# Sliding-window attention and SwiGLU on one core: scores of two heads on the two row halves of the array, 65-column products by 128 keys, in half-head steps

## Chip, cores, metric

One core of one Trainium2 chip. The metric is the device time of one execution in microseconds (us); lower is better. In the profiled runs the time is about 1.7 us more than the span of the profile. Engines in the profile: PE is the TensorE matmul, PEld its weight load, DVE VectorE, ACT ScalarE, POOL GpSimd, SP SyncE.

## The reference

```python
# q, k, v: (8 batches, 8 heads, 576 positions, 64)
scores = q @ k^T / 8;  keep 0 <= query - key < 64, else -1e9
x = softmax(scores) @ v                    # per head, then (4608 tokens, 512)
out = (silu(x @ w_gate) * (x @ w_val)) @ w_out   # 512 -> 1536 -> 512, f32
```

## The kernel before

Tokens go through in groups of 128 (36 groups, g); four groups make a tile t of 512 tokens for the gate and value matmuls. A batch has 576 positions, so every ninth half-group of 64 begins a sequence. All matmuls use bf16 operands, except the turns (transposes through the array) of keys and queries, which the profile shows as f32. Exp needs no running maximum; the row sum comes from a column of ones beside the values.

The attention part. Keys are stored block-diagonally: 64 keys of head a of a pair in rows and columns 64a to 64a+63. One matmul then makes the scores of 64 keys of both heads, with the whole array. The values are block-diagonal too, so that a product has 130 output columns (two heads of 64 and two sums).

```python
    def scores(g):
        E = Es[g % ER]
        m = 2 * g
        ...
        for h in range(2):
            s_ps = ps_a.tile([P, 2, 4, 64], FP32, name="s_ps", tag="a")
            for i in range(2):
                p = 2 * h + i
                nc.tensor.matmul(s_ps[:, i, 0], keys(m + 1, p), queries(m + 1, p))
                nc.tensor.matmul(s_ps[:, i, 1:3], keys(m, p), queries(m, p, 2))
                if g:
                    nc.tensor.matmul(s_ps[:, i, 3], keys(m - 1, p), queries(m, p))
            e = E[:, 1:21].rearrange("r (p y) x -> r p y x", y=5)[:, 2 * h:2 * h + 2, 0:hi, :]
            act.activation(e, s_ps[:, :, 0:hi, :], AF.Exp, scale=0.125)
            dve.tensor_mul(e, e, mk[:, 0:hi].unsqueeze(1).to_broadcast([P, 2, hi, 64]))
```

`ps_a` is a PSUM pool of three one-bank tiles, shared by scores, products, and the turns `tp` (keys, queries) and `xtp` (attention output, the x turns). The gate and value sums have two banks each, the projection one.

`gv` makes the gate and value sums of one of twelve column blocks; its `finish` on DVE comes one step later and frees those two banks:

```python
    def finish(state):
        g_ps, v_ps, th, t, m, c0, n = state
        sg = fsb.tile([P, 512], FP32, name="sg", tag="sg")
        dve.scalar_tensor_tensor(sg[:, 0:n], th[:, 0:n], 1.0, g_ps[:, 0:n], ALU.add, ALU.mult)
        dve.tensor_mul(hT[t][:, m, c0:c0 + n], sg[:, 0:n], v_ps[:, 0:n])
```

The loop, one pass per group, after a written-out prologue that ends with a projection and one more group's attention (cuts: loads and casts):

```python
    flush()
    project(0, 3)
    products(11)
    turn_q(6)
    scores(12)
    turn_x(11)
    ...
    turn_k(7)
    for w in range(8, NG):
        ...
        step(t, 3 * s)                # gv of a block, then finish of the block before
        if w + 4 < NG:
            products(w + 4)
        ...
        step(t, 3 * s + 1)
        if w + 5 < NG:
            scores(w + 5)
        if w + 4 < NG:
            turn_x(w + 4)
        ...
        step(t, 3 * s + 2)
        ...                           # turn_k or turn_q, in turn
        project(t - 1, s)
```

The softmax here doesn't subtract the row's maximum and nothing guards it: scores larger than these inputs give would overflow.

## Time and profile before

| | before |
|---|---|
| time, median of 2 runs | 388.3 us (388.06 to 388.54) |
| span of the profiled run (its own time was 391.72) | 390.0 us |
| PE busy | 364.8 us, 94% |
| DVE, ACT, POOL busy | 67%, 44%, 24% |
| period of the loop, per group | 9.57 us |

The first lines are from the page of the kernel before: busy time of each engine, and the granted matmul clock in 40 slices of the span, in tenths. Then two of its groups of instructions: line, engine, operation, operands, count, then busy us and mean ns of one.

```profile
PE 364.8 (94%) x2524; PEld 209.2 (54%) x2566; DVE 262.1 (67%) x520; ACT 173.1 (44%) x296; POOL 94.5 (24%) x120
...
PEclk9859969999999999999999999999999999999999
...
L162 DVE TENSOR_TENSOR E<-E,mask 128x512 bf16<-128x512 bf16 (+1 forms) x72 | 42.1, 589 | 24.0 <-ACT E L161 21.9
...
L161 ACT ACTIVATE E<-s_ps 128x512 bf16<-128x512 f32 (+1 forms) x72 | 38.7, 594 | 13.9 <-PE s_ps L159 13.0
```

The mean ns of a PE matmul is its latency; matmuls overlap, and the pace is read from the starts. The chain of waits does that. These are lines of the chain of the kernel before, in order of time (start us, us, what), for a little more than one group in the loop.

```profile
212.27 0.86 PE g_ps L235 x4
...
214.00 0.68 PE ao_ps L180 x12
214.68 0.86 PE g_ps L235 x4
...
216.25 0.19 PE s_ps L156
...
216.86 0.22 PE xtp L199 x4
...
218.81 0.44 PE tp L111 x4
219.25 2.59 PE o_ps L252 x12
221.84 0.86 PE g_ps L235 x4
```

One group takes 221.84 - 212.27 = 9.57 us, and nothing but PE stands in the chain. Twelve products take 0.68 us, so 56.6 ns each; the scores take 0.45 us (in the timeline of PE, from the first score at 216.25 us to the first x turn at 216.70; the first score piece of this chain is longer because one value matmul before it is missing from the records). In the stretch from 165 to 300 us PE is busy 134.11 of 135 us. The loop starts at about 117 us; before it the core waits for loads, then for chains of Exp, mask and finish.

### The profile page before, as it was taken

What the parts mean: (1) busy time and instruction counts of PE and PEld (TensorE: products, weight loads), DVE (VectorE), ACT (ScalarE), POOL (GpSimd) and SP (SyncE); (2) the same over time, 40 slices, a digit from 0 to 9 for tenths busy, and PEclk for the clock granted to TensorE, in tenths of its full rate; (3) what the DMA queues carried; (4) which work ended last, traced back from release to release, by engine and by line L of the source; (5) the groups of instructions that cost most, each with busy time, mean ns of one, the idle gap of its engine ahead of it and who ended that gap; (6) DMA issues with size and microseconds to landing.
All of it is one profiled execution on the core that took longest, in us unless ns stands there. A gap on an engine that the chain in (4) does not pass through costs nothing.

```text
span 390.0 us, 6619 instructions
## 1 busy us (share of the span) xinstructions
PE 364.8 (94%) x2524; PEld 209.2 (54%) x2566; DVE 262.1 (67%) x520; ACT 173.1 (44%) x296; POOL 94.5 (24%) x120
## 2 busy tenths in 40 slices
PE   8679698988879999999999999999999999999995
PEld 3464355766655555555555555555555555544442
DVE  6857777856666777675777686768777766664530
ACT  2265539534354454544343434343545444423321
POOL 3702342702145222222222222222222200000000
PEclk9859969999999999999999999999999999999999
DMA  9979999518741525253626352636263100000112
GB/s 204 301 224 233 312 341 208 120 54 165 174 109 44 134 82 134 83 134 89 141 90 141 83 137 85 137 86 143 86 145 85 48 28 29 27 29 28 54 54 83
DMA packets 88320, 47.62 MB, mean 122 GB/s; under 512 B 39136, under 2 KB 82144, under 8 KB 88288
## 3 DMA queue, kind: packets, MB, share of 16 engines
q1 hardware_dynamic: 88288, 47.20, 48.5%
q8 instruction: 20, 0.33, 0.4%
q14 instruction: 12, 0.10, 0.1%
HBM read 37.75 MB, written 9.44 MB: 121 GB/s over the span
## 4 chain that ended last, share of the span: by engine, by line
PE 81%; DVE 8%; DMA 4%; ACT 3%; issue 2%; SPq 1%; POOL 1%; ACTq 0%; POOLq 0%; DVEq 0%
PE o_ps L252 24%; PE g_ps L235 21%; PE v_ps L235 21%; PE ao_ps L180 5%; PE tp L111 4%; DMA k_f<-in_k_dram 2%; PE xtp L199 2%; PE s_ps L157 2%; DVE E L162 2%; ACT E L161 2%; DMA v_f<-in_v_dram 1%; DVE x_b L185 1%; PE s_ps L156 1%; DVE kbd L120 1%; PE s_ps L159 1%
## 5 line engine op out<-in xcount | busy, mean ns | idle before, releaser
L235 PE MATMUL g_ps<-xT,wg 128*128 128x512 bf16 (+1 forms) x457 | 111.6, 358 | 5.9 <-DVE sg L246 3.9
L235 PE MATMUL v_ps<-xT,wv 128*128 128x512 bf16 (+1 forms) x473 | 112.3, 359 | 0.9 <-DVE hT L247 0.5
L240 ACT ACTIVATE th<-g_ps 128x512 f32<-128x512 f32 (+1 forms) x120 | 67.5, 562 | 83.7 <-DVE x_b L185 44.6
L252 PE MATMUL o_ps<-wo,hT 128*128 128x512 bf16 x420 | 96.5, 379 | 0.7
L246 DVE SCALAR_TENSOR_TENSOR sg<-th,g_ps 128x512 f32<-128x512 f32 (+1 forms) x120 | 75.3, 628 | 17.1 <-ACT th L240 16.6
L247 DVE TENSOR_TENSOR hT<-sg,v_ps 128x512 bf16<-128x512 f32 (+1 forms) x120 | 76.1, 634 | 9.7 <-PE ao_ps L180 0.5
L235 PEld LDWEIGHTS <-wv 128*128 128x128 bf16 x480 | 47.1, 98 | 48.4 <-issue 2.2
L252 PEld LDWEIGHTS <-hT 128*128 128x128 bf16 x432 | 42.2, 98 | 45.4
L235 PEld LDWEIGHTS <-wg 128*128 128x128 bf16 x480 | 44.7, 98 | 40.0 <-issue 7.2
L162 DVE TENSOR_TENSOR E<-E,mask 128x512 bf16<-128x512 bf16 (+1 forms) x72 | 42.1, 589 | 24.0 <-ACT E L161 21.9
L104 POOL CAST k_fw<-k_f 128x1024 bf16<-128x1024 f32 x17 | 23.0, 1353 | 125.9 <-DMA k_f<-in_k_dram 87.0
L132 POOL CAST vbd<-v_f 64x512 bf16<-64x512 f32 x72 | 45.6, 634 | 24.1 <-DMA v_f<-in_v_dram 20.7
L184 DVE RECIPROCAL r<-ao_ps 128x4 f32<-128x4 f32 x72 | 12.8, 177 | 51.3 <-PE ao_ps L180 51.2
L161 ACT ACTIVATE E<-s_ps 128x512 bf16<-128x512 f32 (+1 forms) x72 | 38.7, 594 | 13.9 <-PE s_ps L159 13.0
L104 POOL CAST q_fw<-q_f 128x1024 bf16<-128x1024 f32 x17 | 23.2, 1362 | 60.2 <-DMA q_f<-in_q_dram 46.5
L180 PE MATMUL ao_ps<-vbd,E 128*128 128x130 bf16 x428 | 32.5, 226 | 3.7 <-DVE E L162 2.3
L180 PEld LDWEIGHTS <-E 128*128 128x128 bf16 x428 | 28.0, 100 | 12.9 <-DVE E L162 4.0
L185 DVE TENSOR_TENSOR x_b<-ao_ps,r 128x256 bf16<-128x256 f32 x72 | 30.6, 425 | 2.5
L120 DVE COPY kbd<-tp 64x1024 bf16<-64x1024 bf16 x36 | 24.6, 684 | 3.8 <-PE tp L111 3.5
L200 ACT COPY xT<-xtp 128x512 bf16<-128x512 bf16 x36 | 21.3, 591 | 8.5 <-PE xtp L199 8.4
L126 ACT COPY qT<-tp 128x1024 bf16<-128x1024 bf16 x18 | 18.2, 1012 | 13.2 <-PE tp L111 13.2
L156 PE MATMUL s_ps<-qT,kbd 128*128 128x64 bf16 x144 | 20.1, 197 | 3.8 <-ACT qT L126 1.8
(75 smaller groups left out, 216.2 us busy)
## 6 DMA issues: line engine op xcount, KB each, us to landing
v_f<-in_v_dram SPq DMA_DIRECT2D x32, 256.0 KB, 5.3
k_f<-in_k_dram SPq DMA_DIRECT2D x12, 512.0 KB, 4.3
q_f<-in_q_dram SPq DMA_DIRECT2D x12, 512.0 KB, 5.0
w_f<-in_moe_w_gate_dram SPq DMA_DIRECT2D x6, 512.0 KB, 7.1
w_f<-in_moe_w_val_dram SPq DMA_DIRECT2D x6, 512.0 KB, 7.2
wo_f<-in_moe_w_out_dram SPq DMA_DIRECT2D x6, 512.0 KB, 6.7
k_f<-in_k_dram SPq DMA_DIRECT2D x4, 384.0 KB, 4.7
q_f<-in_q_dram SPq DMA_DIRECT2D x4, 384.0 KB, 5.5
```

What stands on the lines that cost most here:

```text
L104: eng.tensor_copy(y, x_f[:])
L120: dve.tensor_copy(kbd[n % KR][h, :, :, 64 * a:64 * a + 64], tp[h].rearrange("r p (b x) -> r p b x", x=64),)
L132: eng.tensor_copy(vbd[n % VR][64 * a:64 * a + 64, c:4:2, :, 64 * a:64 * a + 64], v_f[64 * c:64 * c + 64, :, a:8:2, :],)
L161: act.activation(e, s_ps[:, :, 0:hi, :], AF.Exp, scale=0.125)
L162: dve.tensor_mul(e, e, mk[:, 0:hi].unsqueeze(1).to_broadcast([P, 2, hi, 64]))
L180: nc.tensor.matmul(o_ps[:, i, :], w, x, start=(n == 0), stop=(n == len(parts) - 1))
L185: dve.tensor_mul(x_b[:, 256 * h:256 * h + 256].rearrange("r (p a d) -> r p a d", p=2, a=2), o_ps[:, :, 0:P].rearrange("r p (a d) -> r p a ...
L235: nc.tensor.matmul(ps[:, 0:n], w[:, c, P * m:P * m + P], xT[t][:, c, c0:c0 + n], start=(c == 0), stop=(c == 3),)
L240: act.activation(th[:, 0:n], g_ps[:, 0:n], AF.Tanh, scale=0.5)
L246: dve.scalar_tensor_tensor(sg[:, 0:n], th[:, 0:n], 1.0, g_ps[:, 0:n], ALU.add, ALU.mult)
L247: dve.tensor_mul(hT[t][:, m, c0:c0 + n], sg[:, 0:n], v_ps[:, 0:n])
L252: nc.tensor.matmul(o_ps[:], hT[t][:, c, P * s:P * s + P], wo[:, c, :], start=(c == 0), stop=(c == 11),)
```

## The change

The intent: use row tiling. The keys of a head lie on 64 rows, and two heads of a pair can be multiplied at the same time on the upper and the lower 64 rows of the array, without zeros in between. The scores then come with 128 keys of one head on the partitions, so a product needs two matmuls of 65 columns per head, in place of three of 130 per pair. In this kernel each row half writes to a PSUM tile of its own, so a half of the heads needs two tiles, and the loop takes scores and products in half-head steps (`hs`), both one group earlier than before. For that it puts `scores(13)`, `products(12)` and `turn_q(7)` ahead of the loop. The diff, cut to its core (cut: masks, memsets, casts of v, loads):

```diff
-    VW = 130
+    VW = 65
-    kbd = [cst.tile([P, 4, 4, P], BF16, name=f"kbd{i}") for i in range(KR)]
-    vbd = [cst.tile([P, 4, 4, VW], BF16, name=f"vbd{i}") for i in range(VR)]
-    Es = [cst.tile([P, 21, 64], BF16, name=f"E{i}") for i in range(ER)]
+    kT = [cst.tile([P, 4, 256], BF16, name=f"kT{i}") for i in range(KR)]
+    vb = [cst.tile([P, 2, H, VW], BF16, name=f"vb{i}") for i in range(VR)]
+    Es = [cst.tile([P, H, 256], BF16, name=f"E{i}") for i in range(ER)]
...
+    def scores(g, hs=(0, 1)):
+        prev = m % 9 != 0
+        n = P + 64 if prev else P
+        for h in hs:
+            ps = [ps_a.tile([P, 2, P + 64], FP32, name="s_ps", tag="a") for _ in range(2)]
             for i in range(2):
                 p = 2 * h + i
-                nc.tensor.matmul(s_ps[:, i, 0], keys(m + 1, p), queries(m + 1, p))
-                nc.tensor.matmul(s_ps[:, i, 1:3], keys(m, p), queries(m, p, 2))
-                if g:
-                    nc.tensor.matmul(s_ps[:, i, 3], keys(m - 1, p), queries(m, p))
+                for a in range(2):
+                    nc.tensor.matmul(
+                        ps[a][:, i, 0:P], tokens(kT, g, p, a), tokens(qT, g, p, a),
+                        tile_position=(64 * a, 0),
+                    )
+                if prev:
+                    for a in range(2):
+                        nc.tensor.matmul(
+                            ps[a][:, i, P:n], tokens(kT, g - 1, p, a), tokens(qT, g, p, a, 64),
+                            tile_position=(64 * a, 0),
+                        )
+            for a in range(2):
+                e = E[:, 4 * h + a:4 * h + 4:2, 0:n]
+                act.activation(e, ps[a][:, :, 0:n], AF.Exp, scale=0.125)
+                dve.tensor_mul(e, e, mk[:, 0:n].unsqueeze(1).to_broadcast([P, 2, n]))
...
+            for i in range(4):
+                y = 4 * h + i
+                nc.tensor.matmul(
+                    o_ps[:, i, :], E[:, y, 0:P], vb[g // 2 % VR][:, g % 2, y, :],
+                    start=True, stop=not prev,
+                )
+                if prev:
+                    nc.tensor.matmul(
+                        o_ps[:, i, :], E[:, y, P:2 * P],
+                        vb[(g - 1) // 2 % VR][:, (g - 1) % 2, y, :], start=False, stop=True,
+                    )
...
+    scores(13)
+    products(12)
+    load_v(8)
+    cast_v(7, pool)
+    turn_q(7)
+    pack(8, "k_f", pool)
     for w in range(8, NG):
         step(t, 3 * s)
-            products(w + 4)
+            scores(w + 6, (0,))
+            turn_x(w + 4)
         step(t, 3 * s + 1)
-            scores(w + 5)
-            turn_x(w + 4)
+            scores(w + 6, (1,))
+            products(w + 5, (0,))
         step(t, 3 * s + 2)
+            products(w + 5, (1,))
         ...
         project(t - 1, s)
```

More of the change, by code (lines that the diff above doesn't have):

```diff
@@ L52 @@
     wo = cst.tile([P, 12, DM], BF16, name="wo")
-    kbd = [cst.tile([P, 4, 4, P], BF16, name=f"kbd{i}") for i in range(KR)]
-    vbd = [cst.tile([P, 4, 4, VW], BF16, name=f"vbd{i}") for i in range(VR)]
-    Es = [cst.tile([P, 21, 64], BF16, name=f"E{i}") for i in range(ER)]
+    kT = [cst.tile([P, 4, 256], BF16, name=f"kT{i}") for i in range(KR)]
     qT = [cst.tile([P, 4, 256], BF16, name=f"qT{i}") for i in range(QR)]
-    masks = [cst.tile([P, 4, 64], BF16, name=f"mask{i}") for i in range(3)]
+    vb = [cst.tile([P, 2, H, VW], BF16, name=f"vb{i}") for i in range(VR)]
+    Es = [cst.tile([P, H, 256], BF16, name=f"E{i}") for i in range(ER)]
+    masks = [cst.tile([P, P + 64], BF16, name=f"mask{i}") for i in range(2)]
     ident = cst.tile([P, P], FP32, name="ident")
@@ L114, in turned, with turn_k @@
         )
-    def turn_k(n):
-        tp = turned(n, "k_f")
-        for a in range(2):
-            h = slice(64 * a, 64 * a + 64)
-            dve.tensor_copy(
-                kbd[n % KR][h, :, :, 64 * a:64 * a + 64],
-                tp[h].rearrange("r p (b x) -> r p b x", x=64),
-            )
+    def turn_k(n, eng=None):
+        (eng or dve).tensor_copy(kT[n % KR][:], turned(n, "k_f"))
     def turn_q(n):
@@ L130, in cast_v @@
         for c in cs:
-            for a in range(2):
-                eng.tensor_copy(
-                    vbd[n % VR][64 * a:64 * a + 64, c:4:2, :, 64 * a:64 * a + 64],
-                    v_f[64 * c:64 * c + 64, :, a:8:2, :],
-                )
-    def keys(m, p):
-        return kbd[m // 4 % KR][:, p, m % 4, :]
-    def values(m, p):
-        return vbd[m // 4 % VR][:, m % 4, p, :]
-    def queries(m, p, n=1):
-        o = 64 * (m % 4)
-        return qT[m // 4 % QR][:, p, o:o + 64 * n]
-    def scores(g):
+            eng.tensor_copy(vb[n % VR][:, c, :, 0:D], v_f[:, c])
@@ L148, in scores, with tokens @@
+    def tokens(ring, g, p, a, n=P):
+        o = P * (g % 2)
+        return ring[g // 2 % len(ring)][64 * a:64 * a + 64, p, o:o + n]
+    def scores(g, hs=(0, 1)):
         E = Es[g % ER]
         m = 2 * g
-        mk = masks[1] if m % 9 == 0 else masks[2] if (m + 1) % 9 == 0 else masks[0]
-        hi = 4 if g else 3
-        for h in range(2):
-            s_ps = ps_a.tile([P, 2, 4, 64], FP32, name="s_ps", tag="a")
+        prev = m % 9 != 0
+        n = P + 64 if prev else P
+        mk = masks[1] if (m + 1) % 9 == 0 else masks[0]
+        for h in hs:
+            ps = [ps_a.tile([P, 2, P + 64], FP32, name="s_ps", tag="a") for _ in range(2)]
@@ L154, in scores @@
             for i in range(2):
                 p = 2 * h + i
-                nc.tensor.matmul(s_ps[:, i, 0], keys(m + 1, p), queries(m + 1, p))
-                nc.tensor.matmul(s_ps[:, i, 1:3], keys(m, p), queries(m, p, 2))
-                if g:
-                    nc.tensor.matmul(s_ps[:, i, 3], keys(m - 1, p), queries(m, p))
-            e = E[:, 1:21].rearrange("r (p y) x -> r p y x", y=5)[:, 2 * h:2 * h + 2, 0:hi, :]
-            act.activation(e, s_ps[:, :, 0:hi, :], AF.Exp, scale=0.125)
@@ L162, in scores @@
-            dve.tensor_mul(e, e, mk[:, 0:hi].unsqueeze(1).to_broadcast([P, 2, hi, 64]))
+                for a in range(2):
[9 more added lines that the diff above has]
+                        )
@@ L164, with products @@
+            for a in range(2):
+                e = E[:, 4 * h + a:4 * h + 4:2, 0:n]
+                act.activation(e, ps[a][:, :, 0:n], AF.Exp, scale=0.125)
+                dve.tensor_mul(e, e, mk[:, 0:n].unsqueeze(1).to_broadcast([P, 2, n]))
     xT = {}
     xb = {}
-    def products(g):
-        x_b = att.tile([P, DM], BF16, name="x_b", tag="x_b")
-        E = Es[g % ER][:].rearrange("r y x -> r (y x)")
-        for h in range(2):
-            o_ps = ps_a.tile([P, 2, VW], FP32, name="ao_ps", tag="a")
-            for i in range(2):
-                p = 2 * h + i
-                e = 320 * p
-                parts = [(E[:, e + 128:e + 256], values(2 * g, p))]
-                if g > 0:
-                    parts.append((E[:, e + 256:e + 384], values(2 * g - 1, p)))
-                parts.append((E[:, e:e + 128], values(2 * g + 1, p)))
-                for n, (w, x) in enumerate(parts):
+    def products(g, hs=(0, 1)):
+        if 0 in hs:
+            xb[g] = att.tile([P, DM], BF16, name="x_b", tag="x_b")
+        x_b = xb[g]
+        E = Es[g % ER]
+        for h in hs:
+            o_ps = ps_a.tile([P, 4, VW], FP32, name="ao_ps", tag="a")
+            for i in range(4):
+                y = 4 * h + i
+                prev = 2 * g % 9 != 0
+                nc.tensor.matmul(
[3 more added lines that the diff above has]
+                if prev:
@@ L180, in products @@
                     nc.tensor.matmul(
-                        o_ps[:, i, :], w, x, start=(n == 0), stop=(n == len(parts) - 1)
-                    )
-            r = att.tile([P, 2, 2], FP32, name="r", tag="r")
-            dve.reciprocal(r[:], o_ps[:, :, P:VW])
+                        o_ps[:, i, :], E[:, y, P:2 * P],
+                        vb[(g - 1) // 2 % VR][:, (g - 1) % 2, y, :], start=False, stop=True,
+                    )
+            r = att.tile([P, 4], FP32, name="r", tag="r")
+            dve.reciprocal(r[:], o_ps[:, :, D])
@@ L185, in products @@
             dve.tensor_mul(
-                x_b[:, 256 * h:256 * h + 256].rearrange("r (p a d) -> r p a d", p=2, a=2),
-                o_ps[:, :, 0:P].rearrange("r p (a d) -> r p a d", a=2),
-                r[:].unsqueeze(3).to_broadcast([P, 2, 2, D]),
+                x_b[:, 256 * h:256 * h + 256].rearrange("r (y d) -> r y d", y=4),
+                o_ps[:, :, 0:D],
+                r[:].unsqueeze(2).to_broadcast([P, 4, D]),
             )
-        xb[g] = x_b
     def turn_x(g):
@@ L276 @@
     make_identity(nc, ident[:])
-    dve.memset(kbd[0][:], 0.0)
-    dve.memset(vbd[0][:], 0.0)
     for mk in masks:
@@ L281 @@
     for E in Es:
-        pool.memset(E[:, 0:21:5, :], 0.0)
-    pool.memset(Es[0][:, 4:21:5, :], 0.0)
+        pool.memset(E[:, :, 192:256], 0.0)
     dve.tensor_copy(identb[:], ident[:])
-    for a in range(2):
-        y = slice(64 * a, 64 * a + 64)
+    for y, lo, hi in ((slice(0, P), 0, 63), (slice(P, P + 64), P, -65)):
+        w = y.stop - y.start
+        if lo == 0:
+            pool.affine_select(
+                out=masks[0][:, y], in_=masks[0][:, y], compare_op=ALU.is_ge, fill=0.0,
+                base=0, pattern=[[1, w]], channel_multiplier=-1,
+            )
         pool.affine_select(
-            out=masks[0][y, 0:2], in_=masks[0][y, 0:2], compare_op=ALU.is_ge, fill=0.0,
-            base=0, pattern=[[0, 2], [1, 64]], channel_multiplier=-1,
-        )
-        pool.affine_select(
-            out=masks[0][y, 2:4], in_=masks[0][y, 2:4], compare_op=ALU.is_ge, fill=0.0,
-            base=-1, pattern=[[0, 2], [-1, 64]], channel_multiplier=1,
-        )
-    for i in (1, 2):
-        dve.tensor_copy(masks[i][:], masks[0][:])
-        dve.memset(masks[i][:, 4 - i, :], 0.0)
-    for i in range(VR):
-        if i:
-            dve.memset(vbd[i][:], 0.0)
-        for a in range(2):
-            dve.memset(vbd[i][64 * a:64 * a + 64, :, :, P + a:P + a + 1], 1.0)
+            out=masks[0][:, y], in_=masks[0][:, y], compare_op=ALU.is_ge, fill=0.0,
+            base=hi, pattern=[[-1, w]], channel_multiplier=1,
+        )
+    dve.tensor_copy(masks[1][:], masks[0][:])
+    dve.memset(masks[1][0:64, 64:P], 0.0)
+    for x in vb:
+        dve.memset(x[:, :, :, D:VW], 1.0)
     warm(30)
@@ L305 @@
     pack(0, "q_f", act)
-    for kb in kbd[1:]:
-        dve.memset(kb[:], 0.0)
     cast_v(0, pool)
@@ L453 @@
         step(t, 3 * s)
-        if w + 4 < NG:
-            products(w + 4)
-        if n + 4 < NB:
-            pack(n + 4, "q_f" if odd else "k_f", pool)
-        step(t, 3 * s + 1)
-        if w + 5 < NG:
-            scores(w + 5)
+        if w + 6 < NG:
+            scores(w + 6, (0,))
         if w + 4 < NG:
             turn_x(w + 4)
-        if n + 3 < NB:
-            cast_v(n + 3, pool, (odd,))
-        step(t, 3 * s + 2)
-        if odd and n + 4 < NB:
-            turn_k(n + 4)
-        if not odd and n + 3 < NB:
-            turn_q(n + 3)
-        project(t - 1, s)
-        if odd and n + 5 < NB:
-            load(n + 5, q, "q_f")
-        if not odd:
-            if n + 5 < NB:
+        if odd and n + 5 < NB:
+            pack(n + 5, "k_f", pool)
+        if not odd and n + 4 < NB:
+            pack(n + 4, "q_f", pool)
+        step(t, 3 * s + 1)
+        if w + 6 < NG:
+            scores(w + 6, (1,))
+        if w + 5 < NG:
+            products(w + 5, (0,))
+        if n + 4 < NB:
+            cast_v(n + 4, pool, (odd,))
+        step(t, 3 * s + 2)
+        if w + 5 < NG:
+            products(w + 5, (1,))
+        if n + 4 < NB:
+            if odd:
+                turn_q(n + 4)
+            else:
+                turn_k(n + 4)
+        project(t - 1, s)
+        if n + 5 < NB:
+            if odd:
+                load(n + 5, q, "q_f")
+                load_v(n + 5)
+            else:
                 load(n + 5, k, "k_f")
-            if n + 4 < NB:
-                load_v(n + 4)
     flush()
```

## The prediction

> **What bounds it now.** Busy lines: PE 364.8 of 390.0 us (94%), DVE 67%, ACT 44%, POOL 24%; the chain that ended last is 81% PE. There are two regimes. By stretches, from 165 to 300 us PE is busy 134.1 of 135 us. Its chain repeats every 9.57 us per 128 tokens: six gate/value pieces of 0.86, twelve projection matmuls 2.59, twelve 130-column products 0.68, twelve scores 0.45, four f32 turns 0.44, four x turns 0.22. PE issue is the limit; DVE has about 7.2 us and ACT 4.7 us per period. The first 117 us differ: DMA share 0.9 to 1.0 up to 80 us, granted clock 0.81 to 0.93, and from 60 us the chain also runs through Exp, mask and finish on ACT and DVE.
>
> **What the change moves, per group.**
> - Products: 16 matmuls of 65 columns for 12 of 130. The trace spaces 130 columns 56.6 ns apart and 64 columns 28 ns, weight loads included, so I estimate 16 x 29.5 = 0.47 us: 0.21 us saved. The loop from 117 us holds 24 groups: 5.4 us.
> - Scores: per pair two heads of 128 and 64 columns on row halves. If halves run together: 4 x (56+28) = 0.34 us, 0.11 saved. If weight loads (16, at 28 ns) set the pace: 0.44, nothing saved. If serial: 0.68, 0.23 lost. The Trainium skill, "TensorE: Matmul & The Clock Gate" (Part 3), has row tiles starting about 4 ns apart; "TensorEngine Tiling (Array Packing)", Key Properties, says that changing the tiling mode drains the engine. No trace here shows either. Half-head steps make four changes per group; at an estimated 30 to 60 ns each (a 64-column matmul takes 193 ns, of which 27 is streaming, so 166 is the ceiling) that is 0.12 to 0.24 us, or 3 to 6 us in the loop. I expect 0.45 to 0.6.
> - Exp and mask process 1536 columns instead of 1024, in four instructions (384 wide) instead of two (512). ACT +0.6 to 0.75 us, DVE +0.5; the key copies fall from two of 0.68 per block to one (DVE -0.34 per group). In the loop DVE reaches 7.4 and ACT 5.4 of 9.4 us: off the path.
> - Loop total: 1 to 5 us saved.
>
> **Prologue.** Removing six 0.92 us memsets and the second key copy saves only about 0.5 us: warm-up matmuls hold PE until 10.8 us. Whole-group scores now need four tiles of a three-buffer PSUM pool, so PE waits for an Exp inside each group (estimated 0.5 us), and the Exp-mask chain is about 0.7 us longer. Nine groups lie there: +2 to +5 us against 1.9 us of product savings. scores(13), products(12) and turn_q(7) move ahead of the loop, into a latency-bound spot: +1 us.
>
> **Prediction: 385 us, 377 to 392.** Faster by over 2%: 0.22; within 2%: 0.63; slower: 0.15.
>
> **What would show it.** Loop period 9.2 to 9.5 us; products about 0.47 per group, spaced 29 to 30 ns; both row halves' score matmuls starting within a few ns; gaps of 30 to 60 ns at entry and exit of each score visit; first loop step at or after 118 us (before: 117); PE over 98% busy in the loop.
>
> **What would make it wrong.** Serial row halves, or drains near 166 ns (loop longer, 392 or more); free switches plus a prologue that hides the longer Exp chain (378 or less); PSUM waits in the loop.

## The result

| | before | after |
|---|---|---|
| first runs, median | 388.3 us (388.06 to 388.54, 2 runs) | 398.72 us (398.37 to 399.07, 2 runs) |
| ratio, first runs | | 1.0268, 95% interval 1.0221 to 1.0315 |
| later runs, median | 388.45 us (386.99 to 390.49, 11 runs) | 397.74 us (397.39 to 399.22, 5 runs) |
| ratio, later runs | | 1.0249, 95% interval 1.0218 to 1.0280 |

A ratio is the mean time of one kernel's fast runs over the mean of the other's fast runs of the same rounds, so it is not quite the ratio of the medians. The change makes the kernel slower by 2.5 to 2.7%. The predicted range ended at 392 us.

The page of the kernel after, the lines that answer to those above:

```profile
PE 370.1 (93%) x2752; PEld 197.7 (50%) x2798; DVE 254.2 (64%) x562; ACT 195.9 (49%) x368; POOL 70.3 (18%) x82
...
PEclk9858998999996999999999999999999999999999
...
L158 DVE TENSOR_TENSOR E<-E,mask 128x384 bf16<-128x384 bf16 (+1 forms) x144 | 54.3, 385 | 77.0 <-ACT E L157 74.8
...
L157 ACT ACTIVATE E<-s_ps 128x384 bf16<-128x384 f32 (+1 forms) x144 | 61.1, 477 | 25.1 <-PE s_ps L151 21.8
```

Exp and mask have twice the instructions at three quarters of the width (384 columns for 512). A new dip of the clock stands in the thirteenth slice, at 119 to 129 us. And the chain of waits of the kernel after, for one group in the loop:

```profile
210.81 0.86 PE g_ps L233 x4
...
212.53 0.16 PE s_ps L145 x2
...
212.81 0.33 PE xtp L197 x4
213.14 0.86 PE g_ps L233 x4
...
214.87 0.16 PE s_ps L145 x2
...
215.14 0.14 PE ao_ps L173
...
217.46 0.47 PE tp L113 x4
217.93 2.59 PE o_ps L250 x12
220.52 0.86 PE g_ps L233 x4
```

The period is 220.52 - 210.81 = 9.71 us, 0.14 us more than before, and still nothing but PE stands in it (busy 133.95 of 135 us between 165 and 300 us). Call an unbroken run of score matmuls a visit. The chain puts 0.16 us on the first pair of a visit, 0.33 us on the x turns after the first visit (0.22 before) and 0.14 us on the first product after the second, where the products after it take 0.03 us each. So about 0.1 us of something stands at the entry and the exit of each visit.

To find the other microseconds I use four marks in each trace: the start of the fourth projection (the last before the loop), of the fifth (the first in the loop), of the 32nd (the last in the loop), and the end. Times in us, one trace each; the labels are those of the experiments below.

| kernel | to 4th projection | 4th to 5th | 5th to 32nd | rest | span | loop period |
|---|---|---|---|---|---|---|
| before | 109.7 | 13.9 | 249.2 | 17.2 | 390.0 | 9.57 |
| e1, old layout, new schedule | 107.1 | 16.3 | 247.9 | 16.8 | 388.1 | 9.57 |
| after | 111.4 | 19.3 | 249.9 | 16.8 | 397.4 | 9.71 |
| e9, after again | 110.8 | 18.2 | 249.9 | 16.8 | 395.7 | 9.71 |
| e6, one visit, four tiles, old loop order | 108.6 | 15.9 | 246.5 | 16.8 | 387.8 | 9.47 |

The first trace of before has a long prologue: its own run took 391.72 us, its clock fell between 49 and 58 us (the 6 in the sixth slice above), and e1, with the same instructions up to there, reached the fourth projection 2.6 us sooner. Six traces with one and the same prologue as after (after, e3, e4, e5, e8, e9) reached it between 109.5 and 114.3 us, four of them between 110.6 and 111.6. So single traces fix a prologue to 1 or 2 us at best (e3 lay 3 us off), while the loop repeats to 0.1 us. The means of the fourth projection are 111.4 us for these six and 108.4 us for the two of the old layout (before, e1), 3.0 us apart.

### The profile page after: what moved, and what is told of

It is laid out like the page before. It is cut to its first block, busy times and chain, and to the rows that moved or that the text cites. A ratio compares the mean times of both kernels' runs of the same rounds, so it can differ in the third digit from the quotient of the medians.

```text
span 397.4 us, 7162 instructions
## 1 busy us (share of the span) xinstructions
PE 370.1 (93%) x2752; PEld 197.7 (50%) x2798; DVE 254.2 (64%) x562; ACT 195.9 (49%) x368; POOL 70.3 (18%) x82
## 4 chain that ended last, share of the span: by engine, by line
PE 83%; ACT 5%; DMA 4%; DVE 4%; issue 2%; SPq 1%; POOL 0%; POOLq 0%; ACTq 0%
PE o_ps L250 23%; PE v_ps L233 21%; PE g_ps L233 21%; PE tp L113 4%; PE s_ps L145 4%; PE ao_ps L173 3%; PE xtp L197 3%; DMA k_f<-in_k_dram 2%; ACT E L157 2%; PE w_ps L262 2%; PE ao_ps L178 2%; DVE E L158 2%; DMA v_f<-in_v_dram 2%; DVE x_b L184 1%; PE s_ps L151 1%
## 5 line engine op out<-in xcount | busy, mean ns | idle before, releaser
L233 PE MATMUL v_ps<-xT,wv 128*128 128x512 bf16 (+1 forms) x475 | 114.5, 362 | 0.6
L158 DVE TENSOR_TENSOR E<-E,mask 128x384 bf16<-128x384 bf16 (+1 forms) x144 | 54.3, 385 | 77.0 <-ACT E L157 74.8
L157 ACT ACTIVATE E<-s_ps 128x384 bf16<-128x384 f32 (+1 forms) x144 | 61.1, 477 | 25.1 <-PE s_ps L151 21.8
L145 PE MATMUL s_ps<-qT,kT 64*128 64x128 bf16 x288 | 25.7, 225 | 10.9 <-ACT E L157 5.6
L173 PE MATMUL ao_ps<-vb,E 128*128 128x65 bf16 x288 | 27.3, 201 | 1.8 <-DVE x_b L184 1.5
L145 PEld LDWEIGHTS <-kT 64*128 64x128 bf16 x288 | 14.1, 96 | 28.7 <-issue 26.1
L122 ACT COPY qT<-tp 128x1024 bf16<-128x1024 bf16 x18 | 18.2, 1012 | 17.1 <-PE tp L113 17.0
L173 PEld LDWEIGHTS <-E 128*128 128x128 bf16 x288 | 21.6, 102 | 8.7 <-DVE x_b L184 2.1
L178 PE MATMUL ao_ps<-vb,E 128*128 128x65 bf16 x256 | 25.1, 201 | 0.0
L127 POOL CAST vb<-v_f 128x512 bf16<-128x512 f32 x36 | 22.9, 642 | 7.9 <-DMA v_f<-in_v_dram 7.8
```

The costliest lines, as they stand in the source:

```text
L145: nc.tensor.matmul(ps[a][:, i, 0:P], tokens(kT, g, p, a), tokens(qT, g, p, a), tile_position=(64 * a, 0),)
L157: act.activation(e, ps[a][:, :, 0:n], AF.Exp, scale=0.125)
L158: dve.tensor_mul(e, e, mk[:, 0:n].unsqueeze(1).to_broadcast([P, 2, n]))
L173: nc.tensor.matmul(o_ps[:, i, :], E[:, y, 0:P], vb[g // 2 % VR][:, g % 2, y, :], start=True, stop=not prev,)
L178: nc.tensor.matmul(o_ps[:, i, :], E[:, y, P:2 * P], vb[(g - 1) // 2 % VR][:, (g - 1) % 2, y, :], start=False, stop=True,)
L233: nc.tensor.matmul(ps[:, 0:n], w[:, c, P * m:P * m + P], xT[t][:, c, c0:c0 + n], start=(c == 0), stop=(c == 3),)
```

## The experiments

Two theories stood against each other at first. A: the schedule loses the time, at the way into the loop, where attention work now stands without gate or projection matmuls between and the clock falls to half. B: the layout loses it, by changes of the tiling mode (the array as one block of 128 rows, or as two of 64) and by the longer Exp and mask chain. Each expectation below names its own theories, so the letters A, B and C change their meaning from run to run. The Trainium skill, "TensorEngine Tiling (Array Packing)", Key Properties, says that changing the tiling mode drains the engine, and gives no time for it.

### e1: the new schedule with the old layout

```diff
 # before.py
-    def scores(g):
+    def scores(g, hs=(0, 1)):
-    def products(g):
+    def products(g, hs=(0, 1)):
 # and everything from "turn_k(7)" to the end of the loop as in after
```

> The old layout (two heads' keys block-diagonal, 130-column products, no row halves) in the new schedule: half-head steps in the loop, scores one group earlier, and scores(13), products(12), turn_q(7) ahead of the loop. Theory A (the time was lost at the way into the loop, where this work stands with no projection or gate matmuls between, and the matmul clock falls to half): slower than before by 3 to 6 us, so about 391 to 394 us; the first step of the loop starts 3 to 5 us later than in before, a granted clock below 0.9 between 110 and 130 us, and the loop's period stays 9.57 us. Rival B (the loss is all in the row-half layout: mode switches and the longer Exp and mask chain): within 1 us of before, no dip of the clock at the loop's entry.

Measured: 389.99 us (389.02 to 390.85, 4 runs), 1.0032 of before (0.9994 to 1.0071). The granted clock is 1.00 in every stretch from 50 us on. Theory A in its strong form falls: the schedule alone costs about 1 us, and its interval reaches zero. The work that it moves out of the loop (249.2 - 247.9 = 1.3 us) comes back at the entry with about 1 us on top. The remaining 2.2 to 2.4% (1.0249 and 1.0268 over 1.0032) belong to the layout. By the marks, e9 less e1, so the layout within one schedule: 3.7 us to the fourth projection (with the spread of single prologues), 1.9 us at the entry, 2.0 us in the loop, 7.6 us in all. The medians of the runs agree, though from other rounds: 397.74 - 389.99 = 7.75 us, so with 2.0 us in the loop some 5.7 us lie ahead of it. (The loop loses less than 23 groups times 0.14 us, mostly because the two groups in it that begin a sequence skip the second term of scores and products and take about 0.3 us less each.)

### e2: the same score matmuls on the whole array

Each head's keys on all 128 rows, zeros in the other head's half; no tiling.

```diff
-    kT = [cst.tile([P, 4, 256], BF16, name=f"kT{i}") for i in range(KR)]
+    kz = [[cst.tile([P, 4, 256], BF16, name=f"kz{a}{i}") for i in range(KR)] for a in range(2)]
-                        ps[a][:, i, 0:P], tokens(kT, g, p, a), tokens(qT, g, p, a),
-                        tile_position=(64 * a, 0),
+                        ps[a][:, i, 0:P], tokens(kz[a], g, p, a), tokens(qT, g, p, a),
 # tokens() gives all 128 rows; turn_k copies two halves; the zeros are set once
```

> The kernel after, but each head's keys are padded with zeros to all 128 rows and the matmuls run on the whole array, one after another: same number of score matmuls, same Exp, masks, products, schedule, no tiling. Theory A (the 0.09 to 0.10 us before and after each score visit is the change of the tiling mode): the gaps vanish, a visit takes 4 x 56 + 4 x 28 = 0.34 us in place of 0.37, the loop's period is about 9.65 us in place of 9.71, the total 1 to 2 us below the kernel after (about 397). Rival B (the gaps are waits of the first weight load or for the PSUM tiles, which any such visit pays): the gaps stay, a visit takes 0.5 us or more, the period is 10.0 us and the total 6 us or more above the kernel after.

Measured: 398.34 us (397.96 to 399.33, 4 runs), 1.0256 of before; period 9.63 us. The period is as theory A had it (9.65). The total is 1.3 us above what I expected and level with after, not below it. The trace has a late fourth projection (113.6 us), and this kernel has extra memsets and half copies ahead of it, but 113.6 us lies within the spread of after's own prologue, so the cause of the 1.3 us is not shown. At the way into the loop e2 is about as late as e9 (18.2 us): 18.0 us from the fourth to the fifth projection (e1 16.3), though its clock is 1.00 there and its tiling mode never changes. PE waits 0.49 and 0.55 us for an Exp inside `scores(12)` and `scores(13)`, where e1 has no such wait. So a good part of what the layout loses at the entry is neither clock nor mode. What matters for the loop is the visit itself. First the timeline of PE in the kernel after around the second score visit of a group, then that of e2 (start us, us from the first start to the last end, operands, count).

```profile
213.84 1.03 PE L233 MATMUL v_ps<-xT,wv 128*128 128x512 bf16 x4
214.80 0.23 PE L145 MATMUL s_ps<-qT,kT 64*128 64x128 bf16 x2
214.87 0.19 PE L151 MATMUL s_ps<-qT,kT 64*128 64x64 bf16 x2
214.90 0.22 PE L145 MATMUL s_ps<-qT,kT 64*128 64x128 bf16 x2
214.95 0.19 PE L151 MATMUL s_ps<-qT,kT 64*128 64x64 bf16 x2
215.08 0.20 PE L173 MATMUL ao_ps<-vb,E 128*128 128x65 bf16 x1
```

```profile
213.91 1.03 PE L234 MATMUL v_ps<-xT,wv 128*128 128x512 bf16 x4
214.78 0.28 PE L148 MATMUL s_ps<-qT,kz 128*128 128x128 bf16 x2
214.89 0.22 PE L153 MATMUL s_ps<-qT,kz 128*128 128x64 bf16 x2
214.95 0.28 PE L148 MATMUL s_ps<-qT,kz 128*128 128x128 bf16 x2
215.06 0.22 PE L153 MATMUL s_ps<-qT,kz 128*128 128x64 bf16 x2
215.12 0.19 PE L174 MATMUL ao_ps<-vb,E 128*128 128x65 bf16 x1
```

Four value matmuls at 0.216 us take 0.86 us. In e2 the first score starts 0.87 us after the first of them, with no gap; in after it starts 0.96 us after, a gap of about 0.10 us. At the other end the next matmul is due 28 ns after a 64-column pair starts (the two run together) and comes after 0.13 us: again 0.10 us. In between, the row halves do what they promise: a pair of 128 columns takes 0.23 us from first start to last end, little over the 0.22 us of one matmul, where e2's serial pair takes 0.28. The four pairs of starts span 0.18 us with the halves together and 0.34 us without. The whole visit is 0.38 us against 0.34 us. Rival B (a wait that any visit pays) falls: with the same tiles, order and counts, the gaps are gone when the mode doesn't change. This is no single case: between 165 and 300 us all 28 visits of after start 0.311 or 0.312 us after the start of the matmul before, and all 28 of e2 0.215 or 0.216 us.

The weight loads (PEld) show what the gap holds. In e2 the first load of keys starts at 214.56 us, with the last value matmul, so it is hidden behind it. In after it starts at 214.80 us, together with its own score matmul and 0.31 us after the start of the last value matmul. The busy share cannot show this gap, as the last value matmul is recorded until 214.87 us.

### e3: twice the changes of mode

```diff
-            scores(w + 6, (0,))
+            scores(w + 6, (0,), (0,))   # pair 0 of this half
             turn_x(w + 4)
+            scores(w + 6, (0,), (1,))   # pair 1, then Exp and masks
...
-            scores(w + 6, (1,))
+            scores(w + 6, (1,), (0,))
             products(w + 5, (0,))
+            scores(w + 6, (1,), (1,))
```

> The kernel after with each score visit of the loop cut in two by work that is there anyway (the x turns, the first half of the products): eight changes of the tiling mode per group in place of four, same instructions. Theory A (a change costs about 0.095 us): period 9.71 + 4 x 0.095 = 10.09 us, total +7 to +9 us on the kernel after (about 406). Rival B (the gap is the cost of a visit's first load or wait, hidden when a tile is already open): +0 to +4 us. Rival C (longer Exp and mask chain bounds the loop): also the second half's Exp starts 0.2 to 0.3 us later, so a rise with new PE waits for DVE or ACT rather than gaps around the scores.

Measured: 406.97 us (405.28 to 410.41, 4 runs), 1.0481 of before; period 10.14 us. Four more changes cost 10.14 - 9.71 = 0.43 us, 0.107 us each. The timeline of PE in e3 shows them where the cut was made:

```profile
218.29 0.23 PE L148 MATMUL s_ps<-qT,kT 64*128 64x128 bf16 x2
...
218.48 0.40 PE L202 MATMUL xtp<-identb,x_b 128*128 128x128 bf16 x4
218.81 0.23 PE L148 MATMUL s_ps<-qT,kT 64*128 64x128 bf16 x2
```

Four x turns at about 56 ns would be done after 0.22 us; the next pair starts 0.33 us after the first of them. Rivals B and C fall: the steps around the visits kept their pace, and the rise sits in the gaps. (A gap from x turn to score is 0.152 us from start to start in e3 where x turns follow each other at 0.056, so 0.096 us; about 0.05 us of the 0.43 us per group lies elsewhere.)

### e4: the work at the entry spread over the first two groups

```diff
-    scores(13)
-    products(12)
-    turn_q(7)
+    step(2, 0)
+    products(12, (0,))
+    scores(13, (0,))
+    step(2, 1)
+    products(12, (1,))
+    scores(13, (1,))
+    step(2, 2)
+    turn_q(7)
+    turn_x(12)
 # ... and so on; the loop starts at group 10
```

> The kernel after, with scores(13), products(12) and turn_q(7) taken out of the stretch ahead of the loop and spread over the first two groups' steps, between gate and projection matmuls. Theory A (bubble and cold clock at the way into the loop): first loop step at about 117 to 118 us in place of 122, no clock dip after 117 us, total 4 to 6 us below the kernel after (393 to 395). Rival B (the loss is in the loop): within 1.5 us of the kernel after.

Measured: 397.01 us (396.86 to 397.52, 4 runs), 1.0216 of before, 0.7 to 1.7 us less than after's two medians. The expected 4 to 6 us did not come, and the dip stayed (granted clock 0.66 from 117 to 122 us): the sparse stretch around scores(12), which e4 leaves as it was, seems to be enough for it. Theory A keeps a share of about 1 us.

### e5: the new layout with the old schedule

```diff
 # after.py, with the loop of before (whole-group scores and products), nothing ahead of it
```

> The new layout (row halves, 65-column products, 192-column scores) in the loop order of before: whole-group scores and products, nothing moved ahead of the loop. Theory A (layout is the loss; the half-head steps are there to hide its PSUM waits): prologue as in the kernel after (fourth projection at about 111 us), entry into the loop 14 to 17 us in place of 19.3, but each loop group waits 0.4 to 1 us inside the scores for an Exp to free a tile: period 10.0 to 10.6 us, total 400 to 412. Rival B (the schedule change is what costs): period 9.6 to 9.7 and total within 2 us of before.

Measured: 409.30 us (407.70 to 410.50, 4 runs), 1.0525 of before; period 10.31 us. As expected, this is worse by far: sixteen score matmuls need four PSUM tiles, the pool has three, and PE waits inside the scores until an Exp has read one. The half-head steps were the cure for this, at the price of two more changes of mode per group (e6). The Trainium skill, "TensorEngine Tiling (Array Packing)", Gotcha 1, warns that row tiling raises PSUM pressure because different row tiles write to different banks; this run agrees, at 10.31 - 9.71 = 0.60 us per group above after, and 0.84 us above e6 below, which has four tiles and nearly the same order. The same wait acts in the prologue of after, which keeps whole-group scores. Its PE timeline (idle time before, and who ended it, in brackets) at groups 2 and 3:

```profile
21.27 0.29 PE L145 MATMUL s_ps<-qT,kT 64*128 64x128 bf16 x2 [0.67 <-ACT qT L122]
...
22.32 0.26 PE L145 MATMUL s_ps<-qT,kT 64*128 64x128 bf16 x1 [0.30 <-ACT E L157]
...
23.33 0.26 PE L145 MATMUL s_ps<-qT,kT 64*128 64x128 bf16 x1 [0.36 <-ACT E L157]
...
24.34 0.26 PE L145 MATMUL s_ps<-qT,kT 64*128 64x128 bf16 x1 [0.37 <-ACT E L157]
...
24.81 0.21 PE L173 MATMUL ao_ps<-vb,E 128*128 128x65 bf16 x1
```

The scores of the two groups take 24.81 - 21.27 = 3.54 us from first start to the first product; in before the same stretch went from 21.91 to 23.76, 1.85 us, at the same granted clock of 0.50.

### e6: one visit per group, four tiles

The projection gives up its own bank; its sum, the scores and the rest share a pool of four.

```diff
-    ps_a = ctx.enter_context(tc.tile_pool(name="ps_a", bufs=3, space=PSUM))
+    ps_a = ctx.enter_context(tc.tile_pool(name="ps_a", bufs=4, space=PSUM))
-    ps_o = ctx.enter_context(tc.tile_pool(name="ps_o", bufs=1, space=PSUM))
+        ps = {(h, a): ps_a.tile([P, 2, P + 64], FP32, name="s_ps", tag="a")
+              for h in hs for a in range(2)}       # all sixteen matmuls, then Exp and masks
 # the loop of before: products(w + 4) | scores(w + 5) | turn_x(w + 4) after the third step
```

> As the run before, but a group's sixteen score matmuls stand in one visit, with four PSUM tiles to write to (the projection's bank joins the pool), and the x turns follow the third step: two mode changes per group in place of four. Theory A (a change costs 0.095 us, the sum of matmul streams is the rest): period 9.71 - 0.19 to 0.24 = 9.47 to 9.52 us, 0.05 to 0.1 below before, fourth projection at 109 to 111 us because no score waits for an Exp; total 386 to 391. Rival B (the gap belongs to something else than the change of mode): period 9.65 or more.

Measured: 389.22 us (386.30 to 389.47, 3 fast runs; a fourth of 392.48 us was slow), 0.9987 of before (0.9936 to 1.0038). The period is 9.47 us, and it is seen in two projections of the chain of e6:

```profile
209.59 2.59 PE o_ps L250 x12
...
219.06 2.37 PE o_ps L250 x11
```

That is theory A's figure: two changes fewer than 9.71 give 9.71 - 2 x 0.107 = 9.50, and one tenth of a microsecond less than before. The fourth projection comes at 108.6 us (108.8 in e7, which has the same prologue), earlier than in all six traces of after's prologue (mean 111.4 us). So writing to four tiles in one visit wins back about 2.7 us there. The scores of groups 2 and 3, the stretch shown under e5, take 2.68 us here (20.98 to 23.66), at the same clock of 0.50. The kernel comes level with before, not ahead of it.

### e7: one visit per group in the schedule of after

```diff
 # after.py with the four tiles of e6
         step(t, 3 * s)
-            scores(w + 6, (0,))
-            turn_x(w + 4)
+            scores(w + 6)
         step(t, 3 * s + 1)
-            scores(w + 6, (1,))
+            turn_x(w + 4)
             products(w + 5, (0,))
```

> The kernel after with its schedule, but one visit of sixteen score matmuls per group (four PSUM tiles, as in the run before) in place of two half-head visits. Theory A: period 9.50 to 9.52 us, in place of 9.71, so 4 to 5 us less in the loop, and 1 to 3 us less before it: total 391 to 395. Rival B (gaps not from mode changes): period 9.65 or more, total within 3 us of the kernel after.

Measured: 398.12 us (397.52 to 398.55, 4 runs), 1.0237 of before; period 9.91 us. The expectation was wrong by 0.4 us per group, and the chain of waits of e7 shows why:

```profile
199.86 0.16 PE s_ps L144 x2
...
200.56 1.26 ACT E L157 x3
...
201.84 0.36 DVE E L158
202.20 0.61 DVE sg L244
...
202.85 1.02 PE g_ps L233 x4
```

With all four Exps and masks right after the first step, DVE's in-order queue has four masks ahead of the finish that frees the gate bank, and the third step's gate matmuls wait for it. In e6 the visit follows the second step, the finish of the first step is ahead of the masks, and the finish behind them is needed only after the third step, the turns and a projection (1.73 + 0.22 + 0.44 + 2.59, about 5 us). So the place of a visit counts as much as the number of its mode changes.

### e8: matmuls of zeros at the entry

```diff
     products(11)
     turn_q(6)
+    warm(5)
     scores(12)
     turn_x(11)
+    warm(2)
```

> The kernel after with seven matmuls of zeros added in the sparse stretch ahead of the loop (five after turn_q(6), two after turn_x(11)), whose results nobody reads. Theory A (the half clock from 117 to 125 us comes of that sparse stretch and costs about 2.5 us): no stretch under 0.95 of the clock between 112 and 130 us, total 1.5 to 3 us below the kernel after (396 to 397.5), in spite of more work. Rival B (the dip is not set by activity, or costs nothing): dip stays, total the same or 0.5 to 1.5 us longer.

Measured: 397.27 us (396.70 to 398.26, 4 runs), 1.0219 of before (1.0189 to 1.0250). The dip is gone. The columns below are the stretch, its length, busy us and count of PE, PEld, DVE, ACT, POOL, the granted clock, DMA share and GB/s; first after, then e8.

```profile
112.00:117.00 5.00, 3.38 (x44) 2.09 (x43) 3.11 (x10) 2.24 (x4) 0.00 (x0) 1.00 0.28 74
117.00:122.00 5.00, 4.46 (x51) 3.34 (x52) 4.33 (x10) 3.33 (x8) 1.79 (x2) 0.64 1.16 273
```

```profile
112.00:117.00 5.00, 4.57 (x44) 2.56 (x43) 3.21 (x9) 2.04 (x4) 0.00 (x0) 1.00 0.23 63
117.00:122.00 5.00, 4.29 (x55) 2.94 (x56) 4.40 (x9) 3.83 (x10) 1.85 (x2) 1.00 1.17 278
```

So the dip can be filled. A sparse stretch alone does not make one: before (PE busy 3.33 of 5 us from 112 to 117 us) and e2 (2.79 from 117 to 122) kept a clock of 1.00. The entry went from 19.3 (after) and 18.2 (e9) to 17.6 us. The total is 0.5 to 1.5 us below after's two medians, at the edge of what was expected, and its interval overlaps e9's, so the price of the dip is about 1 us and not well fixed.

### e9: the kernel after again

> The kernel after unchanged, for more fast runs beside the same runs of before: 1.025 to 1.028 of before, period 9.71 us, fourth projection at 110.5 to 112 us, fifth 19 to 19.5 us later, clock dip between 117 and 127 us. If the dip or the early stretch differs from the first trace, how far single traces may be used for the prologue is limited accordingly.

Measured: 397.74 us (397.39 to 399.22, 5 runs), 1.0249 of before. The loop is the same to 0.1 us, the entry 1.1 us shorter than in the first trace with a shorter dip (0.69 from 117 to 122 us, 0.97 after it).

### e10, e11, e12: is there a version that beats both?

e10 is e6 with `project(0, 3)` moved behind `turn_q(6)`, so that it fills the wait for the query copy. e11 is e10 with fifteen matmuls of zeros in the first 30 us. e12 is before with the same move as e10.

```diff
-    project(0, 3)
     products(11)
     turn_q(6)
+    project(0, 3)
     scores(12)
```

> The kernel with one visit per group, four PSUM tiles and the loop order of before (layout_four, 0.9987 of before), with project(0,3) moved behind turn_q(6), so that twelve matmuls stand where PE waited for the query copy. Theory A (the entry into the loop loses about 1 us to that wait and about 1.5 us to the half clock that follows): no clock below 0.95 between 112 and 127 us, total 1.5 to 2.5 us below layout_four: 0.992 to 0.996 of before. Rival B (the entry is bound by the Exp chain whatever PE does): 0.997 to 1.001.

> As the run before, plus fifteen matmuls of zeros in the waits of the first 30 us. Theory A (the new layout's sparser first groups let the clock fall to half until about 34 us, which costs 2 to 3 us): granted clock from 20 to 30 us above 0.8 in place of 0.50, first projection 1 to 2 us earlier, 0.988 to 0.993 of before. Rival B (that stretch waits for DMA and for the Exp chain, so the clock does not matter, or the fillers stand in the way): first projection no earlier, total the same or up to 2 us longer.

> The kernel before with the same move of project(0,3) behind turn_q(6) and nothing else. If the move is worth something by itself, before gains it too: about 1 us from the wait for the query copy, no clock effect as before has no dip there: 0.996 to 0.999 of before. If it gains as much as the new layout does from it, the new layout's edge over before is only the loop's 0.1 us per group, about 2 us in all.

Measured: e10 387.80 us (386.64 to 390.43, 6 runs), 0.9989 of before (0.9956 to 1.0022); e11 389.25 us (6 runs), 1.0020 (0.9988 to 1.0052); e12 388.81 us (6 runs), 1.0012 (0.9981 to 1.0044). None is told from before. In e10's trace the dip is gone, and third to fifth projection take 26.6 us against 29.0 in e6; but the ratio did not follow, so the gain is not shown. The same move does nothing for before: 27.2 us from third to fifth projection in e12, 27.0 in before. e11 answers one question: its clock between 20 and 30 us is 0.84 where e10 has 0.50, and its first projection came no earlier (80.5 against 80.0 us). No gain from the fuller clock of the first 30 us is seen; as the added matmuls themselves stand in PE's queue, this does not prove that the half clock there is free.

## Why the prediction was wrong, point by point

- **What bounds the loop: right.** PE alone stands in the chain before and after, 99% busy.
- **Products: right.** "16 x 29.5 = 0.47 us": the after timeline has eight in 0.24 us, 30 ns each, 0.20 us saved per group.
- **Row halves together: right.** A pair of 128 columns spans 0.23 us where one takes 0.22, which agrees with the start distance of about 4 ns that I took from the Trainium skill, "TensorE: Matmul & The Clock Gate", Part 3: in the packed trace of after the halves of a pair start 3.3 ns apart, the mean between 165 and 300 us. The stream of scores is 0.35 us per group (two visits of about 0.18) for 0.45.
- **The price of a mode change: this is the step that failed in the loop.** "At an estimated 30 to 60 ns each": it is 95 to 107 ns, by the gaps in after and by e3. Four per group cost 0.38 to 0.43 us, where the streams saved 0.20 + 0.10. With 0.05 us more for the two turns (0.24 for 0.22, 0.47 for 0.44) this gives the +0.14 us that the period shows. That a change drains the engine, as the Trainium skill says ("TensorEngine Tiling (Array Packing)", Key Properties), agrees with these gaps; I gave it too small a size, though I had worked out 166 ns as its ceiling. "Loop total: 1 to 5 us saved" became 2.0 us lost (e9 less e1).
- **Prologue: the direction right, the size at or above the upper end.** "+2 to +5 us against 1.9 us of product savings" and 0.5 us from the memsets leaves about 0 to 2.6 us; the means of the traces give 3.0 us (e9 less e1 3.7), and four PSUM tiles in one visit win back about 2.7 of it (e6, e7). In groups 2 and 3 after loses 1.69 us (3.54 less 1.85), of which e6 wins back 0.86. So at least 0.43 us per group is waiting for tiles, which I put at 0.5; these runs do not divide the other 0.4 us per group, nor show how the losses of single groups add up to 3.0 us at the fourth projection. That the longer Exp chain has a part in it is argued, not shown.
- **Entry into the loop: "+1 us".** The move of work by itself did cost that (e1: 2.4 us longer, 1.3 of it moved work). The layout added 1.9 to 3.0 us there; filling the dip won back 0.6 to 1.7 us in the traces. I had not thought of the clock, nor of the waits for PSUM tiles at this place, which e2 shows at a full clock.
- **DVE and ACT off the path in the loop: right** for the half-head order, and e7 shows that this was the order's doing.

The sum: of a forecast of -3 us and a result of about +10, some 5 us is the mode changes in the loop and the rest the prologue and the entry, each 2 to 3 us more than I gave it. With the mode changes priced right the forecast would have been about 390 us, still inside its range; the stretches ahead of the loop carried the result out of it. What stays open: how the entry's loss divides between waits for PSUM tiles, clock and changes of mode; why the clock dips in this sparse stretch and not in those of e2 and before; and whether e10's two microseconds exist.

## What to carry to other kernels

Price a packed matmul by visits, not by columns: each entry to and exit from a tiling mode cost about 0.1 us here, so a visit must save more than 0.2 us of streaming, and one long visit beat two short ones where there were PSUM tiles for it (e6, 9.47 us against 9.71) and the order fitted (it did not in e7, 9.91). Splitting work into half steps to spare PSUM is not free once each half pays that toll; look for a bank first. And when a visit is lengthened or moved, check what its masks or copies now stand ahead of in the in-order queue of the engine that frees the next PSUM bank.

## What the Trainium skill lacked or had wrong

- "TensorEngine Tiling (Array Packing)", Key Properties, says that changing the tiling mode drains the engine, without a size. Here a change between 128 and 64 rows cost 0.095 to 0.107 us at full clock (gaps in after; e3's 0.43 us for four).
- The same page, Performance Considerations, recommends row tiling for contractions of 64 or less without weighing the visit's length. Visits of eight matmuls took 0.38 us tiled and 0.34 us untiled with zero rows (e2).
- "TensorE: Matmul & The Clock Gate", Back-to-back issue gap, gives sustained paces with weight loads of about 81 ns at 128 columns and 131 ns at 512. Here 130 columns with a weight load each went at 56.6 ns, 65 columns at 30 ns, and 512 columns at 216 ns, which fits the formula that the same section keeps for an isolated gap (N / 2.4 + 2.5: 56.7, 29.6 and 215.8 ns).
- The same page, HAM oscillation, names idle gaps over about 3.4 us as what lets the clock fall; the section after it tells of another kernel with frequent short idles, without a size. Here it fell to 0.64 after a stretch whose longest PE wait was 1.10 us (busy 3.38 of 5 us), and it stayed full through equally sparse ones in before (3.33) and e2 (2.79).
